# Attention scores in bursts of four row groups and four PSUM banks, with all other matmuls placed between the bursts

**Chip, cores, metric.** One core of a Trainium2 chip. The metric is the time of one execution on the device in microseconds, the median over fast runs. Times quoted as "span" are of the one profiled execution of a kernel, from its first to its last instruction; they are some 2 us below the medians.

## The reference, cut to what matters

```python
# x: (1, 2048, 512) bf16; 32 heads of 16; window of 256 keys; F = 1376
g = sigmoid((x * gate_w).sum(-1, keepdims=True))
qkv = x @ wqkv
scores = q @ k.T * 16 ** -0.5          # masked: 0 <= query - key < 256
a = softmax(scores) @ v                # per head, then @ wo
b = (silu(x @ w1) * (x @ w3)) @ w2
out = g * a + (1 - g) * b
```

Each block of 128 keys is seen by three blocks of 128 queries: the diagonal one (lower triangle), the next (all of it), and the one after (upper triangle). A head has only 16 dimensions, so the contraction of a score fills a small part of the 128 rows of TensorE's array. Both kernels lay four pairs of heads on the four groups of 32 rows; within a pair, the queries of the other head are set to zero, so that 32 rows give one head's scores.

## The kernel before

The scores of one key block and eight heads come in four tiles of two matmuls (two row groups each); two tiles are in flight. One step of the FFN (the feed-forward network; its matmuls with w1 and w3 are called gate/up here, those with w2 down) stands in the middle of each key block, the other work at its end.

```python
sps = ctx.enter_context(tc.tile_pool(name="sps", bufs=2, space=PSUM))   # score tiles, 2 banks each
pgu = ctx.enter_context(tc.tile_pool(name="pgu", bufs=2, space=PSUM))   # gate/up
pch = ctx.enter_context(tc.tile_pool(name="pch", bufs=2, space=PSUM))   # all other chains
# ... loads: x tile 0, K's weights, Q's weights, x tiles 1, 2, 3, then V's weights, wo, w2, w1, w3
for kb in range(NT):                       # for each of four chunks c of eight heads
    # ... V projection (c == 0), projections of the next chunk
    for i in range(2):
        for up in range(2):
            su = sps.tile([P, 2, 512], F32, name="su")
            for w in range(2):
                r0 = 32 * (2 * up + w)
                nc.tensor.matmul(su[:, w, 0:nq], lhsT=kt_c[r0:r0 + 32, kb * P:(kb + 1) * P],
                                 rhs=qz[r0:r0 + 32, i, q0:q0 + nq], start=True, stop=True)
            eu = epool.tile([P, 2, 3 * P], BF16, name="eu")
            nc.scalar.activation(out=eu[:, :, 0:nq], in_=su[:, :, 0:nq], func=ACT.Exp, scale=SCALE)
            # diagonal mask: GpSimd if up == 0, else DVE; far mask: GpSimd
            if i == 0 and up == 1:
                ffn_catchup(it)
    # ... gate (c == 0)
    if kb >= 1:
        pv_block(c, kb - 1)                # product with V, division, transpose by DMA
    # ... output projection of an earlier tile (last chunk)
```

The builder keeps data dependencies but may move instructions on an engine a little; so the order that counts is the built one.

The softmax here doesn't subtract the row's maximum and nothing guards it: scores larger than these inputs give would overflow.

## Time and profile before

| | before |
|---|---|
| median of the first three runs | 319.5 us |
| median of the 15 runs beside the changed kernel | 318.0 us |
| span of the profiled run | 316.1 us |
| TensorE, ScalarE, DVE, GpSimd busy | 293, 212, 203, 147 us |
| granted TensorE clock, profiled run | 0.992 |

The prediction reads the profile for what bounds the kernel. Columns: line, engine, operation, output and input; busy us, mean ns of one; idle us of the engine before them, and what ended it.

```profile
L339 POOL TENSOR_SCALAR_AFFINE_SELECT eu<-eu 128x256 bf16<-128x256 bf16 x128 | 52.3, 408 | 137.8 <-ACT eu L336 125.7 <-issue 9.9 <-POOL eu L339 1.7
L347 POOL TENSOR_SCALAR_AFFINE_SELECT eu<-eu 128x256 bf16<-128x256 bf16 x224 | 95.6, 447 | 21.9 <-ACT eu L336 21.9
L343 DVE TENSOR_TENSOR eu<-eu,maskA 128x256 bf16<-128x256 bf16 x128 | 41.0, 321 | 50.6 <-ACT eu L336 49.7
```

GpSimd spends 408 ns on a diagonal mask of 256 elements a partition; DVE does the other half of the diagonal masks.

### The profile page before, as it was taken

Reading aid. Unit: us, or ns where it says so; the run is one execution under the profiler, and the core shown is the slowest. Engines: PE = TensorE matmul, PEld = TensorE weight load, DVE = VectorE, ACT = ScalarE, POOL = GpSimd, SP = SyncE. Lnnn points to the kernel's source line nnn. Section 1 sums busy time; section 2 is a strip of 40 time slices with the busy share of each in tenths; the row PEclk is TensorE's granted clock in tenths of the full one; section 3 lists DMA queues with packets and bytes.
Section 4 is the critical chain, followed back from the end, with each engine's and each line's share of the span. In section 5 each row is a group of like instructions: output and inputs, shape, how many; then the busy total and the mean of one; then the engine's idle time right before and its main releaser. Section 6 shows DMA issues by size and latency. Waiting matters only on the chain.

```text
span 316.1 us, 8384 instructions
## 1 busy us (share of the span) xinstructions
PE 293.2 (93%) x3216; PEld 166.7 (53%) x3216; DVE 202.6 (64%) x566; ACT 212.3 (67%) x365; POOL 146.9 (46%) x367
## 2 busy tenths in 40 slices
PE   3389999999999999999999999999999799999993
PEld 2035645555564545656554556566545465556441
DVE  1237867676774467777753777777546577777553
ACT  2045277576785269988973689899845888888530
POOL 5012054544643146666762366666633656665310
PEclk9999999999999979999999999999999999999999
DMA  6993000000000000000000000000000011111101
GB/s 177 360 389 142 0 11 6 9 7 8 10 6 11 4 10 9 10 10 11 10 9 10 10 10 10 11 9 12 11 4 15 10 37 44 44 45 46 42 23 58
DMA packets 19304, 13.16 MB, mean 42 GB/s; under 512 B 10720, under 2 KB 18240, under 8 KB 19264
## 3 DMA queue, kind: packets, MB, share of 16 engines
q1 hardware_dynamic: 19232, 12.63, 12.8%
q8 instruction: 25, 0.41, 0.5%
q0 software_dynamic: 32, 0.00, 0.2%
q14 instruction: 15, 0.12, 0.1%
HBM read 8.42 MB, written 2.10 MB: 33 GB/s over the span
## 4 chain that ended last, share of the span: by engine, by line
PE 75%; ACT 8%; DMA 5%; issue 5%; DVE 2%; POOL 2%; SPq 1%; ACTq 0%; POOLq 0%
PE gu L217 21%; PE su L332 13%; PE chain L234 13%; PE chain L289 9%; PE chain L152 8%; ACT eu L336 8%; PE chain L175 5%; PE chain L270 4%; DMA wqkv_sb<-in_A_wqkv_dram 4%; DMA OT<-ocur 2%; PE chain L141 1%; POOL eu L347 1%; SPq L80 1%; PE chain L357 1%; ACT tt L221 1%
## 5 line engine op out<-in xcount | busy, mean ns | idle before, releaser
L336 ACT ACTIVATE eu<-su 128x768 bf16<-128x768 f32 (+2 forms) x256 | 183.2, 778 | 75.0 <-PE su L332 74.7
L339 POOL TENSOR_SCALAR_AFFINE_SELECT eu<-eu 128x256 bf16<-128x256 bf16 x128 | 52.3, 408 | 137.8 <-ACT eu L336 125.7
L347 POOL TENSOR_SCALAR_AFFINE_SELECT eu<-eu 128x256 bf16<-128x256 bf16 x224 | 95.6, 447 | 21.9 <-ACT eu L336 21.9
L217 PE MATMUL gu<-xT,w_sb 128*128 128x256 bf16 (+1 forms) x704 | 95.7, 274 | 0.0
L343 DVE TENSOR_TENSOR eu<-eu,maskA 128x256 bf16<-128x256 bf16 x128 | 41.0, 321 | 50.6 <-ACT eu L336 49.7
L217 PEld LDWEIGHTS <-w_sb 128*128 128x128 bf16 (+1 forms) x704 | 62.6, 100 | 18.7 <-issue 12.8
L332 PE MATMUL su<-qz,kt 32*128 32x384 bf16 (+2 forms) x512 | 63.0, 322 | 4.4 <-ACT eu L336 3.2
L332 PEld LDWEIGHTS <-kt 32*128 32x128 bf16 x512 | 21.3, 91 | 53.0 <-issue 48.3
L289 PE MATMUL chain<-Vaug,eu 128*128 128x17 bf16 x1440 | 48.1, 171 | 0.7 <-ACT gt L360 0.3
L289 PEld LDWEIGHTS <-eu 128*128 128x128 bf16 x1440 | 41.9, 96 | 10.6 <-issue 8.4
L221 ACT ACTIVATE tt<-gu 128x256 bf16<-128x256 f32 (+1 forms) x88 | 34.1, 391 | 12.7 <-PE gu L217 11.9
L234 PE MATMUL chain<-w_sb,hT 128*128 128x512 bf16 (+1 forms) x176 | 41.8, 380 | 0.0
L152 PE MATMUL chain<-xT,wqkv_sb 128*128 128x512 bf16 x128 | 35.5, 407 | 3.3 <-DVE xT L147 1.9
L225 DVE SCALAR_TENSOR_TENSOR hT<-h,gu 128x256 bf16<-128x256 bf16 (+1 forms) x88 | 36.2, 416 | 2.4
L223 DVE SCALAR_TENSOR_TENSOR h<-tt,gu 128x256 bf16<-128x256 bf16 (+1 forms) x88 | 36.6, 418 | 1.6 <-ACT tt L221 1.3
L234 PEld LDWEIGHTS <-hT 128*128 128x128 bf16 (+1 forms) x176 | 15.7, 97 | 18.2 <-issue 0.9
L236 DVE TENSOR_SCALAR bsb<-chain,omg 128x512 bf16<-128x512 f32 x16 | 12.0, 751 | 19.3 <-PE chain L234 19.3
L295 DVE SCALAR_TENSOR_TENSOR ocur<-chain,gq,rden 128x128 bf16<-128x128 f32 x64 | 22.3, 349 | 1.8
L175 PE MATMUL chain<-wqkv_sb,xT 128*128 128x512 bf16 x64 | 17.9, 409 | 4.0 <-DMA wqkv_sb<-in_A_wqkv_dram 4.0
L152 PEld LDWEIGHTS <-wqkv_sb 128*128 128x128 bf16 x128 | 11.4, 101 | 17.2 <-issue 3.7
L177 DVE CAST Vaug<-chain 128x512 bf16<-128x512 f32 x16 | 11.1, 692 | 12.9 <-PE chain L175 12.9
L270 PE MATMUL chain<-wo_sb,OT 128*128 128x512 bf16 x64 | 16.7, 378 | 2.5 <-DMA OT<-ocur 2.2
(37 smaller groups left out, 104.1 us busy)
## 6 DMA issues: line engine op xcount, KB each, us to landing
w_sb<-in_B_w_dram SPq DMA_DIRECT2D x2, 1376.0 KB, 10.4
xs<-in_A_x_dram SPq DMA_DIRECT2D x4, 512.0 KB, 9.9
out_dram<-ot SPq DMA_DIRECT2D x16, 128.0 KB, 1.9
wqkv_sb<-in_A_wqkv_dram SPq DMA_DIRECT2D x3, 512.0 KB, 8.5
w_sb<-in_B_w_dram SPq DMA_DIRECT2D x1, 1280.0 KB, 10.5
OT<-ocur SPq DMA_TRANSPOSE x64, 2.2
wo_sb<-in_A_wo_dram SPq DMA_DIRECT2D x1, 512.0 KB, 8.5
w_sb<-in_B_w_dram SPq DMA_DIRECT2D x1, 96.0 KB, 9.5
```

Source lines behind the costliest of these rows:

```text
L152: nc.tensor.matmul(ps[:], lhsT=wqkv_sb[:, dc, col0 + c * P:col0 + (c + 1) * P], rhs=xT[:, dc, tq * 512:(tq + 1) * 512], start=(dc == 0), s ...
L217: nc.tensor.matmul(gu[0:fs, wch, :], lhsT=wsb[:, dc, f * P:f * P + fs], rhs=xT[:, dc, t0 + h0:t0 + h0 + 256], start=(dc == 0), stop=(dc == ...
L221: nc.scalar.activation(out=tt[0:fs, :], in_=gu[0:fs, 0, :], func=ACT.Tanh, scale=0.5)
L223: nc.vector.scalar_tensor_tensor(out=h1[0:fs, :], in0=tt[0:fs, :], scalar=1.0, in1=gu[0:fs, 0, :], op0=ALU.add, op1=ALU.mult)
L225: nc.vector.scalar_tensor_tensor(out=hT[0:fs, f, h0:h0 + 256], in0=h1[0:fs, :], scalar=0.5, in1=gu[0:fs, 1, :], op0=ALU.mult, op1=ALU.mult)
L234: nc.tensor.matmul(bps[:], lhsT=hT[0:fs, f, mm * P:(mm + 1) * P], rhs=w2_sb[0:fs, f, :], start=(f == 0), stop=(f == NFC - 1))
L289: nc.tensor.matmul(pva[:, h8, :], lhsT=eu[:, i, col0:col0 + P], rhs=Vaug[:, kp, head, :], start=(bi == 0), stop=(bi == len(blocks) - 1))
L332: nc.tensor.matmul(su[:, w, 0:nq], lhsT=kt_c[r0:r0 + 32, kb * P:(kb + 1) * P], rhs=qz[r0:r0 + 32, i, q0:q0 + nq], start=True, stop=True)
L336: nc.scalar.activation(out=eu[:, :, 0:nq], in_=su[:, :, 0:nq], func=ACT.Exp, scale=SCALE)
L339: nc.gpsimd.affine_select(out=eu[:, :, 0:P], in_=eu[:, :, 0:P], pattern=[[0, 2], [1, P]], compare_op=ALU.is_ge, fill=0.0, base=0, channel_ ...
L343: nc.vector.tensor_tensor(out=eu[:, :, 0:P], in0=eu[:, :, 0:P], in1=maskA[:, None, :].to_broadcast([P, 2, P]), op=ALU.mult)
L347: nc.gpsimd.affine_select(out=eu[:, :, 2 * P:3 * P], in_=eu[:, :, 2 * P:3 * P], pattern=[[0, 2], [-1, P]], compare_op=ALU.is_ge, fill=0.0, ...
```

## The change

Its intent: give TensorE fewer, fuller runs of score matmuls, and measured portions of other work between them. A burst is one such run: matmuls on all four row groups, into four PSUM banks. The text calls it the row mode when TensorE works by groups of 32 rows. The core of the diff, condensed (the old loops that it replaces are above; the list of which piece goes where is cut):

```diff
+    sbig = ctx.enter_context(tc.tile_pool(name="sbig", bufs=1, space=PSUM))   # 4 banks
+    gen = ctx.enter_context(tc.tile_pool(name="gen", bufs=4, space=PSUM))     # 4 banks, all other chains
+    x_dma(0); w_dma(D, 2 * D); w_dma(0, D); x_dma(1); w_dma(2 * D, 3 * D)     # V's weights fifth
+    def exps(dst, big, w):
+        nc.scalar.activation(out=dst[:, :, 0:w], in_=big[:, :, 0:w], func=ACT.Exp, scale=SCALE)
+    def burst_dm(c, kb):                   # diagonal and next block, both heads of each pair
+        big = sbig.tile([P, 4, 512], F32, name="big")
+        for u in range(4):
+            nc.tensor.matmul(big[:, u, 0:2 * n], lhsT=kt[32 * u:32 * u + 32, kb * P:(kb + 1) * P],
+                             rhs=qz[32 * u:32 * u + 32, :, kb * P:kb * P + n], start=True, stop=True)
+        e = dmpool.tile([P, 4, 512], BF16, name="edm")
+        exps(e, big, 2 * n)
+        nc.gpsimd.affine_select(...)       # diagonal mask, 1024 elements a partition
+    def burst_f(c, p):                     # the far blocks of two key blocks: eight matmuls of 256 columns
+        ...                                # exponential, four masks of 512 elements on GpSimd
+    def pv(c, p):                          # product with V for two query blocks, 48 matmuls
+        ...
+    COST = {"proj": 0.87, "v": 0.87, "tx": 0.45, "gate": 0.4, "up": 0.87, "down": 2.38,
+            "out": 0.87, "pv": 1.22}
+    QUANTUM = 2.1
+    for n, (fn, c, a) in enumerate(bursts):            # 92 bursts
+        fn(c, a)
+        # the pieces due after burst n, then FFN pieces until COST adds up to about QUANTUM,
+        # then the product with V and the output projection that are due
```

Gate/up is now done for 256 tokens at a time with two buffers of the hidden tile, the gate is applied at the output instead of at the attention, and GpSimd does all masks.

## The prediction

> **What bounds the kernel now.** I read the page's engine table first, then the chain that ended last, then the groups of instructions by shape, the waits, and the timeline of TensorE.
>
> ```profile
> PE 293.2 (93%) x3216; PEld 166.7 (53%) x3216; DVE 202.6 (64%) x566; ACT 212.3 (67%) x365; POOL 146.9 (46%) x367
> PE 75%; ACT 8%; DMA 5%; issue 5%; DVE 2%; POOL 2%; SPq 1%; ACTq 0%; POOLq 0%
> ```
>
> TensorE is busy 93% of the span, and 75% of the chain that ended last runs over it. ScalarE has a third of its time free. So time must come out of TensorE's own stream.
>
> ```profile
> L332 PE MATMUL su<-qz,kt 32*128 32x384 bf16 x448 | 57.4, 332 | 4.3 <-ACT eu L336 3.2
> L217 PE MATMUL gu<-xT,w_sb 128*128 128x256 bf16 x640 | 87.1, 273 | 0.0
> L336 ACT ACTIVATE eu<-su 128x768 bf16<-128x768 f32 x224 | 169.2, 820 | 49.1 <-PE su L332 48.8 <-issue 0.2
> ACT eu L336 <- PE su L332: 74.7, 56, 13.8
> PE su L332 <- ACT eu L336: 3.2, 13, 0.6
> ```
>
> The mean of a matmul here (332, 273 ns) is its latency, not what it occupies. ScalarE waits 74.7 us for score matmuls, while TensorE waits only 3.2 us for ScalarE: TensorE is the late one. What it occupies is in the starts:
>
> ```profile
> 124.04 0.44 PE L332 MATMUL su<-qz,kt 32*128 32x384 bf16 x4
> 124.41 1.92 PE L217 MATMUL gu<-xT,w_sb 128*128 128x256 bf16 x16
> 126.26 0.34 PE L332 MATMUL su<-qz,kt 32*128 32x384 bf16 x4
> 126.54 0.21 PE L289 MATMUL chain<-Vaug,eu 128*128 128x17 bf16 x2
> ```
>
> From 124.41 to 126.26 are 1.85 us. Over the trace a 256-column matmul follows another after 109 ns, so 15 steps take 1.64 us and the last step, into the score matmuls, takes 0.205: entering costs 0.097 us extra. Four score matmuls on four row groups start 3 to 4 ns apart; the next ordinary matmul comes 264 ns later (126.26 to 126.54), where 384 columns would stream in 160: leaving costs 0.104. The other steps I read off the same way: 512 columns 216 ns, 17 columns (the product with V) 25.7, 128 columns 56.
>
> Summing these steps over the whole trace: all matmuls but the scores occupy 211.2 us (FFN up 76.7, down 38.0, projections 27.6, V 13.8, output 13.6, product with V 36.3, transposes and gate 5.2). The scores occupy 55.2, plus 16.3 for entering them, which happens 172 times; 71.5 in all. Holes take 22.7. First start 4.4, last start to end 4.0, sum 316. The holes at the start and end:
>
> ```profile
> 4.41 1.89 PE L141 MATMUL chain<-ident,xs 128*128 128x128 bf16 x16 [4.41 <-DMA xs<-in_A_x_dram]
> 10.39 1.89 PE L152 MATMUL chain<-xT,wqkv_sb 128*128 128x512 bf16 x4 [1.35 <-DMA wqkv_sb<-in_A_wqkv_dram]
> 16.26 3.59 PE L175 MATMUL chain<-wqkv_sb,xT 128*128 128x512 bf16 x8 [3.98 <-DMA wqkv_sb<-in_A_wqkv_dram]
> 19.79 0.50 PE L332 MATMUL su<-qz,kt 32*128 32x384 bf16 x2
> 312.06 0.39 PE L270 MATMUL chain<-wo_sb,OT 128*128 128x512 bf16 x1 [1.00 <-DMA OT<-ocur]
> ```
>
> The first scores come at 19.79, because V's weights arrive behind three tiles of x; the eight V matmuls then run at half rate (427 ns a step).
>
> **What the Trainium skill says.** "TensorEngine Tiling (Array Packing)", Key Properties: changing the tiling mode drains TensorE. The trace agrees: 0.097 us in and 0.104 out, here paid 172 times. "TensorE: Matmul & The Clock Gate", Part 3: matmuls on different row groups start about 4 ns apart; the trace shows 3 to 4. "ScalarE: Activation LUTs", What ACT_TABLE_LOAD costs: with immediates 186 + 0.833 ns per element, 93 ns less back to back. The trace has 820 for 768 elements (formula 826), 596 for 512 (613), 691 from start to start. "PSUM — Partial Sum Buffer", Specifications: 8 banks. A score burst of four banks and four single banks for all else fill it, so a second burst has no place.
>
> **The change part by part.** (1) Scores come in 92 bursts of 2048 columns over four row groups in four banks (64 diagonal-and-middle, 4 of these half as wide; 28 that pair two far blocks) instead of 256 tiles of two matmuls. Each burst occupies 0.097 + 0.216 + 0.104 = 0.417 us, so 92 give 38.4 minus 0.4 for the four narrow ones: 38. This is on the bounding engine: 71.5 - 38 = 33.5 us less. Of that, 80 fewer mode changes in and out are 16; fewer columns streamed per group about 8; the rest are waits inside score runs.
>
> (2) ScalarE has 92 exponentials in place of 256. 88 of 2048 columns: start to start 691 + 1280 x 0.833 = 1757 ns, duration 1886; 4 of 1024. Sum of durations 170, against 183. Tanh (88) is unchanged. Little moves here in sum, but the order becomes serial: the four-bank tile has one buffer, so the next burst waits for the whole exponential. The trace gives the links: 51 ns from an exponential's end to the matmul released by it; 373 to 433 ns from a 384-column score matmul to its exponential, so some 440 with 512 columns and 10 more for the four starts. The shortest ScalarE cycle is 450 + 1886 + 51 = 2.39 us. A tanh (264 start to start) fits in the 0.5 us while the next burst runs, two just about.
>
> (3) Other TensorE work is cut into pieces of about 2.1 us between bursts. I added the steps in the built instruction order, between each two bursts: 91 stretches, 1.08 to 3.14 us, most 1.85 to 2.3. The cycle of each is the longer of 0.417 + stretch and 2.39. Without ScalarE they sum to 230.2 us, with it to 233.9. So TensorE still bounds, by a hair: 3.7 us lost where a stretch is too short.
>
> (4) DVE loses the multiplication by the mask (128 x 321 ns = 41 us); the product with V is evacuated in pairs. GpSimd takes all masks: 64 of 1024 elements and 112 of 512. From 302 ns (128 elements, the identity) and 408 (256), 0.84 ns per element, they should take 1.05 and 0.62: some 135 us, about as now. Neither is on the path.
>
> (5) V's weights are loaded fourth, behind the second tile of x. That landed at 11.86 before and the transfer behind it at 13.36. Seven V matmuls precede the first burst: 13.4 + 7 x 0.427 = 16.4 against 19.79.
>
> The sum: first burst 16.5; 233.9 to the last burst; 0.2 for it; then 15.5 us of matmuls (two output tiles, the last product with V, seven FFN steps, two downs, two outputs), less the last step 0.2; end 4.0 after the last start as now: 269.9. I add 1 for the last FFN step, whose evacuation the first down waits for, and 5 for what the sum of steps cannot hold: the four general PSUM banks are shared by all chains, and a gate/up tile is now held until an exponential of 1.9 us has passed ScalarE. With 212 such tiles over 92 bursts a bank comes round again after 4 / 2.3 x 2.5 = 4.3 us, while a gate/up tile made just after a burst is held about 3.5 (1.9 exponential, 0.4 tanh, 0.8 DVE, queues). That is tight. So the span is 276. The unprofiled median before is 319.5 for a span of 316.1; carried over in part, 278.
>
> **The rivals.** First, the single score buffer makes ScalarE the bound: every stretch that is long for one engine delays the other and nothing evens it out. For it: the mean TensorE cycle of 2.53 is only 0.14 above 2.39; a tanh late in a stretch, or two, adds 0.1 to 0.3. Against it: ScalarE now waits 74.7 us for scores and its sum falls. If the cycle becomes 2.7, 92 x 0.17 = 15 us more: span 286, time 288. Second, the four general banks or GpSimd become the bound: the last mask before a product with V takes 1.05 us, and some products stand right behind the far burst, which is 0.32 long. If this costs 0.7 us in each of 32 products, 22 us: time 291 together with the base of 269. Against it: the mask's exponential is over before that burst starts, and the masked tile is needed only by the 27th of 48 matmuls. Third, most of this is hidden and the sum of steps holds: span 270, time 271. Fourth, a drain is not saved because TensorE would have been waiting anyway: against it stand 3.2 us of waits. Then only the waits inside runs and the start are gained, some 12 us: 307. I see little for it.
>
> **Range and chances.** The base without hidden costs is 270, both first rivals end near 290. I say 278, with 269 to 290 to hold it 8 times in 10. To be within 2% (over 313) nearly all of the 33 us would have to be lost, which only two rivals together or an unforeseen wait would do.
>
> **What would show it.** TensorE's score matmuls: 92 runs, some 0.42 us of stream each. The first burst at 16 to 17 us, the last at about 250 to 256. The exponential of 2048 columns near 1.89 us. Waits of TensorE for the exponentials below 10 us, spread over many short ones: if they are 20 or more, the first rival holds. Waits of gate/up or product matmuls for DVE or GpSimd of over 8 us would show the second. A far burst of eight matmuls taking more than 0.1 us over the near one would show that two loads on the same row group do not overlap. The prediction is wrong if the mean distance of bursts is not between 2.5 and 2.65 us.

## The result

| | before | changed |
|---|---|---|
| median | 318.0 us (15 runs) | 279.5 us (11 fast runs of 12) |
| ratio | | 0.8773 (0.8744 to 0.8802) |
| span of the profiled run | 316.1 us | 277.5 us |
| sum of steps on TensorE: all but scores | 211.2 us | 211.2 us |
| scores, with entering the row mode | 71.5 us | 39.2 us |
| holes (steps longer than their kind, over 20 ns) | 22.7 us | 17.2 us |

Waits inside and just behind a run of scores are counted in the row of scores: 10.2 us before (5.5 of them for an exponential to free a score tile) and 0.6 after. So of the 32.3 us by which this row falls, 9.6 are such waits, and the other 22.7 are mode changes and streaming.

A ratio is the mean time of one kernel's fast runs over that of the other's of the same rounds, so it is not quite the ratio of the medians. One run of the changed kernel took 1308 us, at a granted clock of 1.0; it counts as slow and is left out everywhere, and its cause is not known. The fast runs lie from 277.4 to 279.9 us. Steps are times from one matmul's start to the next one's, as in the prediction. The spans leave 2.3 and 1.4 us over these sums (with the first start at 4.4 and 4.5 us and 4.0 after the last start): gaps too short to be counted.

A small part of the gain came with the clock, of which the prediction says nothing. In the profiled run before, the granted clock was 0.5 from 113.2 to 116.6 us, where a step of 512 columns took 427 ns instead of 216; that cost about 1.7 us. In the changed kernel it stood at 1.0 from 15.5 us to the last matmul. Of the runs of the kernel before whose clock is on record, those at a clock of 0.997 and more took 315.4 to 317.6 us, those at 0.989 and less 316.6 to 319.9; the fast runs of the changed kernel had 0.998 to 1.0. Why the clock fell is open.

The engine table and the chain that ended last, after:

```profile
PE 260.6 (94%) x3184; PEld 162.2 (58%) x3184; DVE 163.1 (59%) x366; ACT 200.2 (72%) x189; POOL 143.0 (52%) x189
PE 68%; ACT 17%; issue 4%; DMA 3%; POOL 3%; DVE 2%; SPq 1%; ACTq 0%
```

TensorE's share is as high as before, over a shorter span: it is still the bound, with less work. ScalarE has a larger part of the chain (17%, where it had 8% before). The waits behind that, after (us in total, times, longest):

```profile
ACT edm L218 <- PE big L226: 43.1, 45, 9.6
PE g L270 <- POOL edm L232: 2.1, 6, 0.5
PE big L226 <- ACT edm L218: 0.8, 1, 0.8
```

The timeline of TensorE after, two bursts with an FFN piece between them:

```profile
205.25 0.40 PE L226 MATMUL big<-qz,kt 32*128 32x512 bf16 x4
205.58 2.03 PE L185 MATMUL g<-xT,w_sb 128*128 128x256 bf16 x17
207.69 0.40 PE L226 MATMUL big<-qz,kt 32*128 32x512 bf16 x4
208.02 1.05 PE L185 MATMUL g<-xT,w_sb 128*128 128x256 bf16 x8
```

From burst to FFN matmul 0.33 us, as in the prediction's terms 0.216 + 0.104 and the starts. From 205.58 to 207.69 are 2.11 us for 17 steps: 16 x 0.109, the last with entering 0.206, and 0.16 of hole. That hole is ScalarE's floor: the exponential of the burst at 205.25 ran from 205.76 for 1.88 us, to 207.64, and 51 ns later the next burst started. The whole cycle is 2.44 us. 35 of the 91 cycles stand on this floor (2.42 to 2.45 us); their mean is 2.66.

The rows of exponentials and masks, after:

```profile
L218 ACT ACTIVATE edm<-big 128x2048 bf16<-128x2048 f32 x60 | 112.7, 1878 | 41.2 <-PE big L226 40.7
L232 POOL TENSOR_SCALAR_AFFINE_SELECT edm<-edm 128x1024 bf16<-128x1024 bf16 x64 | 70.5, 1102 | 78.0 <-ACT edm L218 77.6 <-ACT gt L169 0.3
L250 POOL TENSOR_SCALAR_AFFINE_SELECT ef<-ef 128x512 bf16<-128x512 bf16 x112 | 67.9, 638 | 38.3 <-ACT ef L218 37.0 <-ACT gt L169 1.3
```

And the wait that is new, a product with V that stands around a far burst. TensorE, then GpSimd:

```profile
82.50 0.40 PE L243 MATMUL big<-qz,kt 32*128 32x256 bf16 x8
82.83 0.26 PE L270 MATMUL g<-Vaug,edm 128*128 128x17 bf16 x4
83.47 0.54 PE L270 MATMUL g<-Vaug,edm 128*128 128x17 bf16 x15 [0.39 <-POOL edm L232]
```

```profile
82.32 1.10 POOL L232 TENSOR_SCALAR_AFFINE_SELECT edm<-edm 128x1024 bf16<-128x1024 bf16 x1 [1.71 <-ACT edm L218]
```

The mask ends at 83.42, and only then the product goes on (83.47). Measured from start to start such holes sum to 3.8 us; the list of waits shows less, as it counts an engine as idle only after its modelled end.

The start and the end, after:

```profile
12.68 3.08 PE L156 MATMUL g<-wqkv_sb,xT 128*128 128x512 bf16 x7 [1.10 <-DMA wqkv_sb<-in_A_wqkv_dram]
15.69 0.40 PE L226 MATMUL big<-qz,kt 32*128 32x512 bf16 x4
...
257.87 0.29 PE L226 MATMUL big<-qz,kt 32*128 32x256 bf16 x4
...
272.82 1.03 PE L208 MATMUL g<-wo_sb,OT 128*128 128x512 bf16 x4
```

The first scores come at 15.7 instead of 19.8 us, the last burst starts at 257.9, and the last four matmuls follow each other without the wait of 1.0 us for a transpose that stood there before.

### The profile page after: what moved, and what is told of

It is laid out like the page before. It is cut to its first block, busy times and chain, and to the rows that moved or that the text cites.

```text
span 277.5 us, 7493 instructions
## 1 busy us (share of the span) xinstructions
PE 260.6 (94%) x3184; PEld 162.2 (58%) x3184; DVE 163.1 (59%) x366; ACT 200.2 (72%) x189; POOL 143.0 (52%) x189
## 4 chain that ended last, share of the span: by engine, by line
PE 68%; ACT 17%; issue 4%; DMA 3%; POOL 3%; DVE 2%; SPq 1%; ACTq 0%
PE g L185 16%; ACT edm L218 16%; PE g L201 14%; PE g L270 11%; PE g L142 8%; PE big L226 7%; PE g L156 5%; DMA wqkv_sb<-in_A_wqkv_dram 3%; PE g L208 3%; POOL edm L232 3%; PE big L243 2%; ACT tt L189 1%; DVE h L191 1%; PE g L121 1%; DVE hT L193 0%
## 5 line engine op out<-in xcount | busy, mean ns | idle before, releaser
L218 ACT ACTIVATE edm<-big 128x2048 bf16<-128x2048 f32 x64 | 116.8, 1825 | 43.6 <-PE big L226 43.1
L232 POOL TENSOR_SCALAR_AFFINE_SELECT edm<-edm 128x1024 bf16<-128x1024 bf16 x64 | 70.5, 1102 | 78.0 <-ACT edm L218 77.6
L185 PE MATMUL g<-xT,w_sb 128*128 128x256 bf16 (+1 forms) x704 | 89.4, 273 | 0.0
L250 POOL TENSOR_SCALAR_AFFINE_SELECT ef<-ef 128x512 bf16<-128x512 bf16 x112 | 67.9, 638 | 38.3 <-ACT ef L218 37.0
L191 DVE SCALAR_TENSOR_TENSOR h<-tt,g 128x256 bf16<-128x256 bf16 (+1 forms) x88 | 35.3, 418 | 52.2 <-ACT tt L189 51.9
L218 ACT ACTIVATE ef<-big 128x2048 bf16<-128x2048 f32 x28 | 52.6, 1877 | 9.3 <-PE big L243 9.2
L270 PE MATMUL g<-Vaug,edm 128*128 128x17 bf16 x992 | 42.9, 171 | 2.3 <-POOL edm L232 2.1
L270 PEld LDWEIGHTS <-edm 128*128 128x128 bf16 x992 | 39.3, 96 | 5.4 <-POOL edm L232 3.0
L201 PE MATMUL g<-w_sb,hT 128*128 128x512 bf16 (+1 forms) x176 | 41.2, 380 | 0.0
L270 PE MATMUL g<-Vaug,ef 128*128 128x17 bf16 x448 | 38.1, 171 | 0.0
```

The lines of the kernel that those rows point to most:

```text
L185: nc.tensor.matmul(gu[0:fs, wch, :], lhsT=wsb[:, dc, f * P:f * P + fs], rhs=xT[:, dc, t * 256:(t + 1) * 256], start=(dc == 0), stop=(dc == ...
L191: nc.vector.scalar_tensor_tensor(out=h1[0:fs, :], in0=tt[0:fs, :], scalar=1.0, in1=gu[0:fs, 0, :], op0=ALU.add, op1=ALU.mult)
L201: nc.tensor.matmul(ps[:], lhsT=hT[0:fs, f, (m % 2) * P:(m % 2 + 1) * P], rhs=w2_sb[0:fs, f, :], start=(f == 0), stop=(f == NFC - 1))
L218: nc.scalar.activation(out=dst[:, :, 0:w], in_=big[:, :, 0:w], func=ACT.Exp, scale=SCALE)
L232: nc.gpsimd.affine_select(out=tri, in_=tri, pattern=[[0, 4], [0, 2], [1, P]], compare_op=ALU.is_ge, fill=0.0, base=0, channel_multiplier=-1)
L250: nc.gpsimd.affine_select(out=tri, in_=tri, pattern=[[0, 4], [-1, P]], compare_op=ALU.is_ge, fill=0.0, base=-1, channel_multiplier=1)
```

## The experiments

The theory: TensorE's stream sets the time, and a run of scores costs what the starts show (entering, streaming, leaving). The main rivals: the gain comes from ScalarE's fewer, larger exponentials; or ScalarE's chain through the single score buffer is what now sets every cycle. All runs here gave correct results; one of the four times of run 4 was slow. The granted clock of the profiled runs was 0.989 or more, but for run 4. In some traces about 1% of TensorE's records are missing; no hole quoted here is one of those.

**1. One more mode change per burst** (e1_mode_twice).

```diff
+        for i in range(2):                 # halves of columns instead of all at once
+            if i == 1:                     # one ordinary matmul between; its result is overwritten
+                nc.tensor.matmul(big[:, 0, n:n + 1], lhsT=ident[:], rhs=gwc[:, 0:1], start=True, stop=True)
             for u in range(4):
-                nc.tensor.matmul(big[:, u, 0:2 * n], ..., rhs=qz[32 * u:32 * u + 32, :, kb * P:kb * P + n], ...)
+                nc.tensor.matmul(big[:, u, i * n:(i + 1) * n], ..., rhs=qz[32 * u:32 * u + 32, i, kb * P:kb * P + n], ...)
+        # cut: the far burst gets the same matmul between its two sets of four
```

> The changed kernel with one ordinary one-column matmul put into the middle of each burst, between its first and second half of columns. All four row groups still stream at once; what is added is one more leaving and entering of the row mode per burst: 0.104 + 0.025 + 0.097 = 0.226 us. Theory (TensorE's own stream sets the time, mode changes cost what the starts show): both the TensorE cycle and the ScalarE cycle grow by 0.226, so 92 x 0.226 = 20.8 us more, less up to 2 that waits for masks give back: 298 (296 to 301). Rival (mode changes hide behind the exponentials, the gain came from elsewhere): under 5 us more, below 285.

Measured: 296.5 us, ratio to before 0.9333 (0.9283 to 0.9382), so 17.0 us over the changed kernel. TensorE's timeline in this run:

```profile
227.28 0.29 PE L229 MATMUL big<-qz,kt 32*128 32x256 bf16 x4
227.50 0.18 PE L226 MATMUL big<-gwc,ident 128*128 128x1 bf16 x1
227.61 0.29 PE L229 MATMUL big<-qz,kt 32*128 32x256 bf16 x4
227.83 0.61 PE L185 MATMUL g<-xT,w_sb 128*128 128x256 bf16 x4
```

A burst now lasts 0.55 us to the next ordinary matmul, where it was 0.327: 0.223 more, as expected. Over the trace the steps in bursts grew by 20.3 us and the span by 17.3; the difference is holes that shrank (masks 3.8 to 1.7 us). So 92 more mode changes in and out, with the one-column matmuls (2.3 us) that make them, cost 17 us of time; they are not hidden behind the exponentials. One thing this run cannot tell: a longer burst also starts its exponential later, so it lengthens ScalarE's cycle as much as TensorE's. Which of the two sets the time is tested in run 8.

**2. Two pairs of row groups one after the other** (e2_two_pairs).

```diff
         for u in range(4):
             dst = big[:, u, 0:2 * n]
+            if u == 2:
+                nc.tensor.matmul(big[:, 2, 0:1], lhsT=ident[:], rhs=gwc[:, 0:1], start=True, stop=True)
             nc.tensor.matmul(dst, ...)     # the far burst likewise
```

> The changed kernel with the one-column matmul put between row groups 0, 1 and row groups 2, 3 of each burst: the two pairs no longer run beside each other, as in most score runs of the kernel before. Theory: one more mode change (0.226 us) and one more stream of 512 columns (0.216), 0.442 us for each of 92 bursts, 40.7 us: 318 to 320, which gives the whole gain back. Rival (the gain is fewer and larger exponentials on ScalarE, whose number is unchanged here): it stays below 295.

Measured: 312.6 us, ratio 0.9839 (0.9782 to 0.9895), 33 us over the changed kernel. A burst in this run:

```profile
240.66 0.39 PE L229 MATMUL big<-qz,kt 32*128 32x512 bf16 x2
240.98 0.18 PE L227 MATMUL big<-gwc,ident 128*128 128x1 bf16 x1
241.09 0.39 PE L229 MATMUL big<-qz,kt 32*128 32x512 bf16 x2
241.41 0.61 PE L185 MATMUL g<-xT,w_sb 128*128 128x256 bf16 x4
```

It lasts 0.75 us instead of 0.327. The steps in bursts grew by 38.2 us, the holes shrank by 4.7. I had put the steps at 40.7 and not taken off the shrinking holes, so the expectation was some 6 us high; but of the gain of 38.5 us only about 5 are left, with exponentials, masks and order of loads untouched. So the gain does not come from fewer and larger exponentials: it hangs on the length of the bursts, that is on four row groups at once and few changes of mode. That the length counts through TensorE, and not through ScalarE's cycle, is again left to run 8.

**3. V's weights earlier, alone, in the kernel before** (e4_before_v_early).

```diff
-    for t in range(1, NTC):
-        x_dma(t)
+    x_dma(1)
     nc.sync.dma_start(out=wqkv_sb[:, :, 2 * D:3 * D], ...)
+    for t in range(2, NTC):
+        x_dma(t)
```

> The kernel before with V's weights loaded behind the second tile of x instead of the fourth: the part of the change at the start, alone. Theory: V's matmuls start at 13.4 instead of 16.3, the first scores at about 16.9 instead of 19.8, and as TensorE never catches up this stays to the end: 2.9 us less, ratio to before 0.991. Rival (the start is hidden, later waits take it up): within 0.5 us of before.

Measured: 315.1 us, ratio 0.9919 (0.9889 to 0.9949). In its trace the V matmuls start at 12.43 and the first scores at 15.96 us. The first scores come 3.8 us earlier, and 2.6 us (by the ratio, 1.6 to 3.5) are left of that at the end. So the part of the start is real, a few us of the whole.

**4. Four row groups at once in the kernel before** (e5_before_four).

```diff
-    sps = tc.tile_pool(name="sps", bufs=2)
+    sps = tc.tile_pool(name="sps", bufs=1)
             for i in range(2):
+                su4 = sps.tile([P, 4, 512], F32, name="su")
                 for up in range(2):        # four matmuls, then two exponentials
```

> The kernel before with its score tile as one buffer of four banks: four score matmuls of 384 columns on four row groups belong together, two exponentials follow. Exponentials, masks and the order of loads stay as before. In the built order 137 runs of scores instead of 172, 122 of them of four. Theory: TensorE's stream is 35 x 0.2 us of mode changes and the waits inside runs (9.8 us) shorter, but the single buffer gives ScalarE a floor of 1.99 us per run of four; the longer of the two, added up over the built order, is 271 us between first and last run (252 for TensorE alone), plus 20 at the start, 4 of matmuls and 4 at the end: 299. So about half of the whole gain comes without larger exponentials or other masks. Rival (the large exponentials and the other masks bring the gain): it stays above 312.

Measured: 339.1 us, ratio 1.0629 (1.0544 to 1.0714). Both the expectation and the rival missed. Scores with entering fell from 71.5 to 62.6 us, where the theory counted 17 us less; 13.7 of the 62.6 are waits just behind a run of scores, so the matmuls themselves and the mode changes did get shorter (61.3 us before, 48.9 here, without the waits). The holes rose from 22.7 to 48.5. Waits in this run:

```profile
PEld L289 <- POOL eu L342: 17.4, 47, 1.0
PE gu L217 <- DVE hT L225: 11.1, 14, 1.0
```

In the order that the builder made for this tile, products with V and gate/up matmuls stand interleaved, just behind what they wait for. The granted clock was lower too: 0.966 in the profiled run and 0.947 to 0.966 in all four, with 13.7 us at half clock between 246 and 311 us of the trace, where the kernel before has 3.4. So this run does not tell what the bursts alone are worth: the edit changed more than one thing, and the rest cost more. That a single score buffer needs placed work between the bursts is suggested by it, not shown.

**5. The product with V one burst later** (e6_pv_later), to test the new wait for the mask.

```diff
-            n = b0 + 3 * p + (2 if p < NP - 1 else 3)
+            n = b0 + 3 * p + 3
             must[n].append(("pv", pv, (c, p)))
```

> The changed kernel with each product with V placed one burst later. In the trace of the changed kernel TensorE waits 3.8 us in the product for the diagonal mask on GpSimd. Theory: the mask then has a whole further cycle (over 2.4 us against its 1.1), the wait goes, and since TensorE's stream is the bound the time falls by it: the longer-of-two sums over the built order are the same (251.0 against 251.2 from first burst to last matmul), so 279.5 - 3.8 = 275.7. Rival (the waits for masks only stand where TensorE would wait for the exponential anyway): less than 1 us gained.

Measured: 275.7 us, ratio 0.8673 (0.8638 to 0.8708); the interval does not meet that of the changed kernel (0.8744 to 0.8802). The wait was on the path, whole: in this trace no hole behind the diagonal mask is left.

**6. The same wait, made shorter** (e3_mask_half_dve).

```diff
-        nc.gpsimd.affine_select(out=tri, in_=tri, ...)
+        nc.gpsimd.affine_select(out=tri[:, 0:2], in_=tri[:, 0:2], ...)
+        nc.vector.tensor_tensor(out=tri[:, 2:4], in0=tri[:, 2:4], in1=maskA[...], op=ALU.mult)
```

> The changed kernel with half of each diagonal mask on DVE (a multiplication, as the kernel before had) and half on GpSimd. Theory: GpSimd is done after about 0.64 instead of 1.10 us, DVE after about 0.55, so the 3.8 us of waits shrink to about 0.5 and the time to 276.5; DVE's 64 x 0.55 = 35 us more stay hidden (59% busy before). Rival (DVE is what holds the general PSUM banks, and reading SBUF beside GpSimd slows both): no gain or a loss, 279.5 or more.

Measured: 276.4 us, ratio 0.8707 (0.8672 to 0.8742). The holes behind the mask fell from 3.8 to 0.9 us. GpSimd's half took 819 ns, not 0.64 us (512 elements take it 638 in the changed kernel), and DVE's 462 instead of 0.55 us. So GpSimd was slower than reckoned, as the rival had it; whether from DVE working beside it or from the shape of the half is not shown. It was still done early enough. Two different cures give the same 3 to 4 us, so the cause is shown.

**7. Longer exponentials** (e8_exp_quarters), against the rival that ScalarE sets every cycle.

```diff
-        nc.scalar.activation(out=dst[:, :, 0:w], in_=big[:, :, 0:w], func=ACT.Exp, scale=SCALE)
+        for u in range(4):
+            nc.scalar.activation(out=dst[:, u:u + 1, 0:w], in_=big[:, u:u + 1, 0:w], func=ACT.Exp, scale=SCALE)
```

> The changed kernel with each exponential cut into four of 512 columns: 3 x 51 ns = 0.153 us more on ScalarE per burst, 14 us in all, nothing else. Theory (TensorE bounds, ScalarE only where a stretch is short): the built order gives longer stretches now; the sum of the longer of the two is 251.1 with a floor of 2.58 us, against 251.2, so at most 2 us more: 279.5 to 281.5. Rival (the single score buffer makes ScalarE's chain the bound of every cycle): 14 us more, 293.

Measured: 303.2 us, ratio 0.9537 (0.949 to 0.9584): 24 us more, over both. But not from ScalarE:

```profile
PE g L272 <- POOL edm L234: 17.2, 31, 0.8
```

The builder had put products with V right behind bursts whose masks came late (this row was 2.1 us in the changed kernel), and another 7.2 us of holes stand before output matmuls that wait for transposes (after: none). The run is inconclusive on the rival, and was repeated on top of run 5, where the products come later.

**8. Longer exponentials with the products later** (e10_later_quarters): the edits of 5 and 7 together.

> The run with exponentials in quarters again, now on top of the kernel with the products with V one burst later. The first run of quarters came to 303 us, over both theories; its trace shows why it told nothing on ScalarE: in the order that the builder made for it, TensorE waited 17 us in the products for masks that came later. With the products later those waits should be gone, and what is left is the shortest ScalarE cycle, measured there at 2.62 us instead of 2.43. Theory (TensorE bounds, ScalarE only where a stretch is short): the longer-of-two sum over the built order is 254.5 with a floor of 2.62, against 251.0, so 3.5 us over the 275.7 without quarters: 279. Rival (ScalarE's chain bounds every cycle): 92 x 0.19 = 17 us more, 293.

Measured: 278.1 us, ratio 0.8749 (0.871 to 0.8788): 2.5 us over run 5, not 17. In its trace the mask waits are gone and TensorE's holes before bursts sum to some 6.5 us, against 4.5 in the changed kernel. The list of waits for exponentials, in this run:

```profile
PE big L245 <- ACT edm L219: 0.9, 6, 0.2
PE big L228 <- ACT ef L219: 0.6, 1, 0.6
PE big L228 <- ACT edm L219: 0.4, 2, 0.2
```

ScalarE's chain does not set every cycle; it takes its toll only where a stretch of TensorE is short. This also settles what runs 1 and 2 left open: 0.19 us more on every ScalarE cycle costs 2.5 us, so the 17 and 33 us that longer bursts cost there came by TensorE's stream, but for the 4.5 us of holes before bursts at most.

**9. Three general banks** (e9_gen3).

```diff
-    gen = tc.tile_pool(name="gen", bufs=4)
+    gen = tc.tile_pool(name="gen", bufs=3)
```

> The changed kernel with three instead of four general PSUM banks. The prediction added 5 us because four seemed tight (a bank comes round every 4.3 us, a gate/up tile is held about 3.5). With three it comes round every 3 / 2.3 x 2.66 = 3.5 us. Theory (the banks were near their limit): 285 or more, with new holes of TensorE behind DVE's evacuation of gate/up tiles. Rival (they have room; the extra time lies elsewhere): below 281.

Measured: 287.0 us, ratio 0.9036 (0.8996 to 0.9077), 7.5 us more. Behind DVE's evacuation of gate/up tiles stand 6.8 us of holes and 2.4 more right behind bursts, where the changed kernel has 0.7. Their largest row in the list of waits, which counts less:

```profile
PE g L185 <- DVE hT L193: 3.6, 6, 1.0
```

So four banks are enough here, three are not.

**10. A version meant to beat both** (e7_pv_later_q22): run 5 with QUANTUM = 2.2.

> A version that should beat both kernels: the changed kernel with the products with V one burst later and 2.2 instead of 2.1 us of ordinary matmuls aimed at between bursts, so that fewer stretches are shorter than ScalarE's cycle and fewer matmuls are left behind the last burst (6.8 us instead of 12.2). Theory: the longer-of-two sum to the last matmul is 250.0 against 251.0: 274.7, if the last output matmuls do not wait for their transposes. Rival (the shorter end exposes the transposes of the last product, 2.2 us from issue to landing): no gain, 275.7 to 277.

Measured: 277.5 us, ratio 0.8739 (0.8706 to 0.8773): the rival, even a little above it, and no better than run 5. Holes between bursts did fall to 3.7 us; but at the end:

```profile
PE g L208 <- DMA OT<-ocur: 2.8, 2, 1.9
```

Nothing was left to do while the last product was transposed (3.5 us from start to start).

**11. The same with an end that is covered** (e12_later_mixed): QUANTUM 2.2, and 2.0 from three quarters of the bursts on.

> The run before this one closed the holes between bursts (holes of TensorE in the middle 3.7 us) but waited 3.5 us at the end for the transposes of the last product. This one aims at 2.2 us between bursts for the first three quarters of the bursts and at 2.0 in the last, so that one FFN step, two downs and their outputs (10.6 us of matmuls in all behind the last burst) are left to cover the transposes. Theory: the longer-of-two sum is 250.0 as there, without the 3.5 us: ratio to before 0.862 to 0.866, 274. Rival (2.2 us is no better than 2.1 once the end is covered, as the exponentials' floor is already met): 275.7 to 276, ratio 0.867.

Measured: 276.0 us beside 319.0 for the kernel before, ratio 0.8643 (0.8602 to 0.8684). The wait at the end is down to 0.9 us; another of 1.1 us for such a transpose has come up at 217.1 us, right behind a burst. Its interval overlaps that of run 5 (0.8638 to 0.8708): whether it is any better is open. Both lie 1 to 1.5% below the changed kernel by their ratios to before (0.867 and 0.864 against 0.877).

## Why the prediction was right

It said 278.0 us, with 269 to 290; measured were 279.5. Its mechanism was that time must come out of TensorE's own stream, by fewer mode changes and fuller bursts, with ScalarE's cycle just short enough. That held. Step by step:

- **Scores**: 38 us said, 39.2 measured; a burst lasts 0.327 us to the next ordinary matmul instead of 0.320. Runs 1, 2 and 8 together show that this term is what most of the gain is made of. Its three parts were 16 (mode changes), 8 (streaming) and the rest of 33.5 (waits inside runs); those waits, with the ones just behind a run, measured 9.6 us less.
- **Far bursts**: they might have cost more than 0.1 us extra, as two loads fall on each row group. They last 0.331 against 0.327 us.
- **ScalarE's cycle**: 2.39 us said, 2.43 measured. The exponential was 8 ns shorter, the link from the burst's first matmul to its exponential 0.50 instead of 0.45 us.
- **Sum from first to last burst**: 233.9 said, 242.2 measured. The text said the prediction would be wrong if the mean distance were not between 2.5 and 2.65 us; it is 2.66, a hair outside. Of the 8.3 us, 3.8 are the wait for the mask, about 0.8 more waiting for exponentials than the 3.7 said, 1.2 stand in the row of scores (0.6 for the bursts' own length, 0.6 one wait behind a burst), and some 1.7 are waits for DVE; 0.8 are left over. That is why the last burst started at 257.9, past the 250 to 256 that were said.
- **The 5 us for shared banks**: the size served, the cause was wrong. What stood in their place was mostly the second half of the second rival, the mask on GpSimd: part (4) called it off the path, and the rival put it at 22 us. It costs 3.8 us. The argument against it was that the exponential is over before the far burst starts and that 26 matmuls of the product do not need the mask. In three of the ten waits all 26 do stand behind the burst, and the argument fails by tenths: the burst starts 0.05 us after the exponential's end, is 0.33 long, the 26 take 0.67, together 1.05; the product can go on 1.22 us after the exponential's end (0.07 to the mask's start, 1.10 for it, 0.06 to the matmul). These waits are 0.17, 0.17 and 0.24 us. In the other seven (0.25 to 0.68 us, 3.2 of the 3.8) the builder had put the first 3 to 21 matmuls of the product in front of the burst, as at 82 us above, so that fewer than 26 were left to fill the time. The prediction did not see that. That the banks are near their limit is true of three (run 9), not of four.
- **Start and end**: first burst at 16.5 said, 15.7 measured; from the last burst to the end 20.5 said (with 1 for the last FFN step), 19.6 measured; in run 3 the earlier start alone left a gain of 2.6 us. The last FFN step was not waited for: the holes after the last burst are 0.03 us.
- **GpSimd**: masks of 1.05 and 0.62 us said, 1.10 and 0.64 measured.
- **Slips of reading**: the sum that the prediction gives for the span before (316) is 313.8 by its own terms; the missing 2.3 us are gaps too short to be listed. "TensorE waits only 3.2 us for ScalarE" is from the list of waits, which counts from modelled ends; from start to start it is 9.1 us, 5.5 of them inside score runs. Leaving the mode costs 0.101 us (317 less 216 ns for 512 columns, 210 less 109 for 256), not 0.104: the 160 ns for 384 columns in the prediction is no measured step, and the steps of 256 and 512 put it at 162. V's weights are the fifth load, not the fourth. The first rival's 15 us count from a cycle of 2.53, while its base of 270 already holds 2.57, so it is some 4 us too high. None of these carries the result.

That 278 came so close is in part luck: the base of 269.9 was 7.6 us too low (8.3 longer between bursts, 0.8 earlier at the start, 0.1 longer at the end), and the 6 us added for other reasons, the banks and the last FFN step, happened to be nearly the right size. What was worked out well is the large term.

## What to carry to other kernels

Where one engine is busy all the time, add up its steps from start to start by kind, not its busy time. Here that showed that a run of matmuls on row groups pays 0.2 us for entering and leaving the mode, so that few full runs beat many half ones. With a single buffer between two engines, compare the longer of the two for each stretch, not the two sums, and place consumers one full cycle behind a helper engine (run 5). Leave some work for the end, so that the last transposes have something beside them; and when an experiment changes the built order, look at its waits and its granted clock before believing its time.

## What the Trainium skill lacked or had wrong

- "TensorEngine Tiling (Array Packing)", Key Properties, says that a change of mode drains TensorE, without a cost. Here it is 0.097 us to enter and 0.101 to leave, and 0.223 per burst for one more pair with a one-column matmul (0.025) in between (run 1).
- "TensorE: Matmul & The Clock Gate", Part 3, says under "What overlaps and what doesn't" that a weight load overlaps matmuls in flight only when the row groups differ; under "The mechanism" it also allows a load into the background weight buffer. The second is what the far bursts of the changed kernel fit: the second load on a row group starts some 11 ns after the first matmul on that group, and the second set of four matmuls starts 109 ns after the first (256 columns), so the load is hidden. A burst with two sets takes 0.331 us, one with a single set of the same columns 0.327.
- The same page, Back-to-back issue gap, gives about 131 ns a matmul for 512 columns in a real stream of loads and matmuls. Here such a stream takes 216 ns for 512, which fits the page's formula for the isolated gap, as 109 for 256 does. The 25 ns for 17 columns do not fit that formula (9.6), but the floor of about 25 ns that the page's Part 1 states.
- "GPSIMD Engine Reference" has no duration for an affine select. Here, bf16 in place: 302 ns for 128 elements a partition, 408 or 447 for 256 (diagonal and far mask), 638 for 512 (819 in run 6), 1102 for 1024.
- "ScalarE: Activation LUTs", What ACT_TABLE_LOAD costs, says that activations back to back overlap by about 93 ns. Here it is some 120: exponentials of 768 elements take 811 (median) and start 690 apart where they follow at once, those of 2048 take 1877, and a tanh starts 1757 after the start of one at the least. Its formula for the duration itself holds over four PSUM banks in one instruction: 1892 ns for 2048 elements, measured 1878.
